# Pooling six key chunks of one batch by row sums, one of them on GpSimd, and one more GELU chunk on VectorE, in a kernel of attention and a feed-forward layer

## The chip, the cores and the metric

The kernel runs on one core of a Trainium2 chip. The metric is device time in microseconds of one execution; lower is better. Three runs of the kernel before took 941.83, 941.97 and 942.03 us, so its median is 941.97 us.

## The reference

Attention with spatially reduced keys, followed by a feed-forward layer with a fast GELU (all inputs float32):

```python
# q (4, 12288, 128), kv (4, 384, 32, 128), w_sr (128, 128)
kv_pool = kv.reshape(B, H // 4, 4, W // 4, 4, C).mean(axis=(2, 4))
k = v = kv_pool.reshape(B, -1, C) @ w_sr            # 768 keys in each batch
a = softmax(q @ k.T / sqrt(C));  x = a @ v          # 49152 tokens of 128
h = x @ w_in                                        # d_ff = 2048
out = (h * sigmoid(1.702 * h)) @ w_out
```

## The kernel before

**Tiles.** The 49152 tokens are cut into 96 groups of 512. A group of attention has 6 chunks of 128 keys (`JC`), a group of the feed-forward layer ("MoE" in the names) 16 chunks of 128 hidden units (`FCH`). A *chunk* is always a 128x512 piece: TensorE makes it in PSUM by one matmul of 512 columns (a *fill*: L404 in attention, L690 in MoE), ScalarE puts three chunks (two at the start) through exp or GELU in one ACTIVATE (L406, L692) and writes them in bf16 into a ring `ag` of 102 chunks, and TensorE reads them back (a *drain*: L418 in attention, 4 matmuls of 129 columns a chunk, and L700 in MoE, one matmul of 512 columns). The ring lets drains lag behind fills by many chunks. Normalised attention outputs (L446, L449 on VectorE) go into the SBUF tile `x`, tile by tile of 2048 columns, to DRAM and back transposed.

**Order.** The program runs attention of groups 0 to 47, MoE of 0 to 47, attention of 48 to 95, MoE of 48 to 95. A planner in Python (the loop at the end, with `now`, `end`, `free`, `dve`) writes out one fixed order for every engine: in each step it fills the next two or three chunks, and then puts drains and small jobs (`extras`, `early_fill`) into TensorE's queue as long as by its costs they fit ahead of the next fill. Each engine works its queue in that order, and waits on semaphores where data is not there.

**Chunks that ScalarE does not do.** 36 exp chunks and the 27 GELU chunks of `lent` are computed on VectorE by polynomials (`early_exp`, `lent_gelu`: 16 VectorE instructions for one GELU chunk) out of a bank that one fill (L475) wrote; the result lies in `aside` and is drained like any other. Of the 27, six are of the first MoE (groups 3, 6, 7, 10, 12, 18).

**Keys of batch 1**, around the change. Each of its six key chunks is a [128, 2048] piece of `kv`, loaded by GpSimd's DMA queue (`load_chunk`, three at group 10, three at group 12). The 4x4 pooling of a chunk is done in one of two ways.

- *In rows*: chunks 0 to 4 (`ADDED`) are loaded as float32 into borrowed homes of 4 KB a partition and more (`homes`: the tile `kvs`, the tile `w_both` of the weights to come, and pairs of tiles of `x`). `add_row` sums them on VectorE in three adds (two at L165, float32, 512 elements a partition; one at L167, to bf16), and `pool_added` then does four small matmuls against `sum4` (L178).
- *By TensorE alone*: chunk 5 is loaded as bf16 into one tile of `x`, and `pool_chunk` does sixteen such matmuls (L154).

`SUM` says at which group each chunk's sums begin. Behind either way stands `key_and_value` (L199, L200), which needs the pooled chunk. GpSimd works one queue: gates (a MEMSET at L600 that waits for one of VectorE, so that loads aren't issued too early), DMA issues (L142, L145, L248), and, for the first 30 token tiles, the normalising multiply (L449).

Of the kernel before, what the change touches and what calls it, by code (L numbers as in the profile page):

```python
# [7 lines left out]
F32 = mybir.dt.float32  # L8
F32R = mybir.dt.float32r
I32 = mybir.dt.int32  # L10
BF = mybir.dt.bfloat16
AF = mybir.ActivationFunctionType
AX = mybir.AxisListType
ADD = mybir.AluOpType.add
# [12 lines left out]
def kernel(  # L27
    ctx, tc, q, kv, w_sr, moe_w_in, moe_w_out, out,
):
    nc = tc.nc  # L30
    B, N, C = q.shape
    _, H, W, _ = kv.shape
    r = 4
# [4 lines left out]
    FCH = d_ff // 128  # L38
    scale = 1.0 / (C ** 0.5)
    G = 512  # L40
    SG = 4 * G
# [21 lines left out]
    R = 2  # L63
    XS = NS // R
    EARLY = 4
    ADDED = (0, 1, 2, 3, 4)
    AG = 102

    cpool = ctx.enter_context(tc.tile_pool(name="const", bufs=1))
# [20 lines left out]
    def acc(key=None):  # L90

        nonlocal last_acc
        last_acc = next_acc()
        turns.append(last_acc)
        turns.remove(last_acc)
        if key:
            closes[last_acc] = key
        return banks[:, last_acc, :]
# [15 lines left out]
    x = xpool.tile([128, XS * SG], BF, name="x")  # L114

    def x_tile(s):
        return x[:, s % XS * SG:(s % XS + 1) * SG]
# [5 lines left out]
    kv_tiles, kv_sums, pooled, pTs, kTs, vs, added = {}, {}, {}, {}, {}, {}, {}  # L123
    kvs = kvsum.tile([128, 2, Wp, C], F32, name="kvs")
    w_both = cpool.tile([128, 2 * d_ff], BF, name="w_both")
    homes = [kvs.rearrange("p a w c -> p (a w c)"), w_both.bitcast(F32)]
    homes += [x[:, s * SG:(s + 2) * SG].bitcast(F32) for s in (XS - 6, XS - 4, XS - 2)]
    wide = dict(zip(ADDED, homes))
    plain = [jc for jc in range(JC) if jc not in wide]
    spots = {jc: XS - 1 - (JC if len(wide) == JC - 1 else k) for k, jc in enumerate(plain)}  # L130
# [7 lines left out]
    def load_chunk(b, jc):  # L138

        a, ch = divmod(jc, HC)  # L140
        if b and jc in wide:
            nc.gpsimd.dma_start(out=wide[jc], in_=kv_r[b, a, ch])  # L142
            return
        t = x_tile(spots[jc] if b else XS - 1 - jc)
        nc.gpsimd.dma_start(out=t, in_=kv_r[b, a, ch])  # L145
        kv_tiles[b, jc] = t.rearrange("p (wp w1 c) -> p w1 wp c", w1=r, c=C)

    def pool_chunk(b, jc):

        ps = acc()  # L150
        t = kv_tiles.pop((b, jc))
        for wp in (0, 2, 1, 3) if (b, jc) == (0, 0) else range(4):
            for w in range(r):
                nc.tensor.matmul(ps[:, 32 * wp:32 * wp + 32], t[:, w, wp, :], sum4,  # L154
                                 start=(w == 0), stop=(w == r - 1))
        pTs[b, jc] = kvtmp.tile([128, 128], BF, name="pTc", bufs=2)
        nc.vector.tensor_copy(pTs[b, jc], ps[:, 0:128])

    def add_row(jc):

        last, wp = False, None
        t = wide[jc].rearrange("p (wp e) -> p wp e", wp=r)
        narrow_sum = wide[jc].bitcast(BF).rearrange("p (wp e) -> p wp e", wp=r)[:, :, 4 * C:5 * C]
        for m in (0, 2):
            nc.vector.tensor_tensor(t[:, m:m + 2, 0:2 * C], t[:, m:m + 2, 0:2 * C], t[:, m:m + 2, 2 * C:4 * C], ADD)  # L165
            yield 3.2
        nc.vector.tensor_tensor(narrow_sum, t[:, :, 0:C], t[:, :, C:2 * C], ADD)  # L167
        added[jc] = narrow_sum
        extras.extend([(pool_added, 1, jc), (key_and_value, 1, jc)])
        last = True  # L170
        yield 3.3
# [34 lines left out]
    def add_kv(b, n):  # L206
        i, w = divmod(n, r)
        if n == 0:
            kv_sums[b] = kvs[0:Hp]
        for i2 in range(2):  # L210
            nc.gpsimd.dma_start(out=kv_sums[b][:, i2], in_=kv_p[b, i, w, :, i2],  # L211
                                **({"accum_op": ADD} if n else {}))
# [33 lines left out]
    def cast_q(s, lo=0):  # L246
        sl = slice(s * SG + lo * G, (s + 1) * SG)
        nc.gpsimd.dma_start(out=q_bf[sl, :].rearrange("(p i) c -> p (i c)", p=128),  # L248
                            in_=q_flat[sl, :].rearrange("(p i) c -> p (i c)", p=128))

    def load_qT(s):
        qTs[s] = qpool.tile([128, 1, SG], BF, name="qT")
        nc.vector.memset(qTs[s][:, 0, 0:1], 0.0)
        nc.sync.dma_start_transpose(out=qTs[s], in_=q_bf[s * SG:(s + 1) * SG, :])


    def load_rest(s, lo):
        qTs[s] = qpool.tile([128, 1, SG], BF, name="qT")
        nc.vector.memset(qTs[s][:, 0, lo * G:lo * G + 1], 0.0)
        nc.sync.dma_start_transpose(out=qTs[s][:, :, lo * G:], in_=q_bf[s * SG + lo * G:(s + 1) * SG, :])  # L260
# [59 lines left out]
    for m in range(0, 128, 32):  # L320
        p = slice(m, m + 32)
# [60 lines left out]

    early = range(NG // R, NG // R + EARLY)
    rolling = [(i, JC - 1) for i in (28, 41, 42, 55, 59, 64, 70, 71, 74, 85, 91, 94)]
    lent = [(g, FCH - 1) for g in (3, 6, 7, 10, 12, 18, 52, 54, 56, 57, 61, 62, 64, 67, 68, 71, 73, 75, 77, 79, 82, 84, 85, 88, 90, 92, 93)]
    turn = [("a",) + c for c in rolling if c[0] < early[0]] + [("m",) + c for c in lent if c[0] < early[0]]
    turn += [("a",) + c for c in rolling if c[0] > early[-1]] + [("m",) + c for c in lent if c[0] > early[-1]]
    aside = agpool.tile([128, K, 512], BF, name="aside")
# [96 lines left out]
    def new_raw():  # L485
        nonlocal raw
        raw = qpool.tile([128, 1, SG], BF, name="qT")[:, 0, 0:2 * G].bitcast(F32)
# [89 lines left out]
    def put_away(n, m):  # L577
        size = PART // 2 if n == 0 and m > FIRST + 1 else PART
        for o in range(m * PART, m * PART + PART, size):
            lo = n * XS * SG + o * T  # L580
            nc.sync.dma_start(out=x_bf[lo:lo + size * T, :].rearrange("(k p) c -> p k c", p=T),
                              in_=x[:, o * T:(o + size) * T].rearrange("p (k c) -> p k c", k=size))

    def bring_back(n, m):
        o = m * PART
        lo = n * XS * SG + o * T
        nc.sync.dma_start_transpose(out=x[:, o * T:(o + PART) * T].unsqueeze(1), in_=x_bf[lo:lo + PART * T, :])
# [7 lines left out]
    def gate():  # L595

        one = gate_tile[:, gates[0] % 8:gates[0] % 8 + 1]
        gates[0] += 1
        nc.vector.memset(one, 0.0)  # L599
        nc.gpsimd.memset(one, 0.0)  # L600
# [6 lines left out]
    def background(i):  # L607

        first_round = i < GB * 2
        s = TURN.get(i, NS) if first_round else i // 4 + 3 if i % 4 == 0 else NS  # L610
        if s < NS:
            load_qT(s)
        if i == 5:
            load_rest(2, 2)
        if i in CAST:
            gate()
            for s in CAST[i]:
                cast_q(s)
        if i in (10, 12):
            gate()  # L620
            for jc in range(i % 10 * 3 // 2, i % 10 * 3 // 2 + 3):
                load_chunk(1, jc)
        for jc in SUM.get(i, ()):
            if jc in wide:
                sums.append(add_row(jc))
            else:
                extras.extend([(pool_chunk, 1, jc), (key_and_value, 1, jc)])
        if i in (28, 33, 38):
            put_away(0, (i - 28) // 5)
        if i in (31, 36, 41):  # L630
            bring_back(0, (i - 31) // 5)
        if i == 40:
            new_raw()
        if 4 * XS - LEAD <= i < 4 * XS:
            gate()
            add_kv(2, i - 4 * XS + LEAD)
        if i == 28:
            gate()
            nc.gpsimd.dma_start(out=w_in_sb, in_=moe_w_in)
        if i == 29:  # L640
            gate()
            nc.gpsimd.dma_start(out=w_out_sb, in_=moe_w_out.rearrange("(o p) c -> p o c", p=128))

    def background_moe(g):
# [16 lines left out]
        if g == 43:  # L661
            raw = None
            background(early[0])
# [19 lines left out]
    extras = []  # L683
# [66 lines left out]
    for n in range(R):  # L750
        part = [c for c in chunks if c[0] // (NG // R) == n]
        while part:
            m = sizes.pop(0) if sizes else K
# [12 lines left out]
        while flat:  # L766
            m = K if len(flat) > sum(rest) else rest.pop(0)
# [36 lines left out]
    def prepare(p):  # L804
# [12 lines left out]

    first = {
        0: [(pool_chunk, 0, 0), (transpose_q, 0), (warm, 1), (key_chunk, 0, 0), (transpose_q, 1)],
        1: [(value_chunk, 0, 0), (warm, 1)],  # L820
        2: [(pool_chunk, 0, 1), (warm, 2), (key_and_value, 0, 1), (warm, 1), (transpose_q, 2)],
        3: [(transpose_q, 3), (transpose_q, 4), (transpose_q, 5)],
        6: [(pool_chunk, 0, 2)],
# [65 lines left out]
    for n in range(len(seq)):  # L889
        fill(n + 2)  # L890
        jobs(n + 3)
        while True:
# [37 lines left out]
            kind, i, c = source[0]  # L930
# [58 lines left out]
```

## Time and profile before

| what | us |
|---|---|
| median of 3 runs | 941.97 |
| the profiled execution | 942.05 |
| its span, first to last instruction | 940.3 |
| TensorE busy | 928.5 |
| ScalarE busy | 927.7 |
| VectorE busy | 620.3 |
| GpSimd busy | 76.0 |

The profiled execution took 942.05 us, 1.75 us more than its span and 0.08 us more than the median. TensorE's and ScalarE's rows both read 99%; what that means is taken up stage by stage below. Groups in the profile are named by line, engine and operation; "128x1024" is 128 partitions by 1024 elements, so two chunks.

### The profile page before, as it was taken

How to read it: one execution, taken by the hardware profiler on the slowest of the kernel's cores; microseconds unless marked ns; L12 is line 12 of the kernel's file. 1: busy time of each engine (PE TensorE's matmuls, PEld its weight loads, DVE VectorE, ACT ScalarE, POOL GpSimd, SP SyncE). 2: the span in 40 equal slices, each digit the busy share in tenths (PEclk: the TensorE clock that was granted, in tenths of full speed). 3: DMA queues.
4: the chain of work that ended last, by engine and by line, in shares of the span. 5: the costliest groups of instructions: out<-in, count | busy, mean ns of one | idle time of the engine just before them, and what ended most of it. 6: DMA issues, size and time to landing. Idle time of an engine off the chain costs nothing.

```text
span 940.3 us, 15356 instructions
## 1 busy us (share of the span) xinstructions
PE 928.5 (99%) x6103; PEld 499.7 (53%) x6218; DVE 620.3 (66%) x1244; ACT 927.7 (99%) x721; POOL 76.0 (8%) x129
## 2 busy tenths in 40 slices
PE   8999999999999999999999999999999999999998
PEld 5777775444444444454447777744444444444444
DVE  6776556685288777777036767457587778577781
ACT  6999999999999999999999999999999999999998
POOL 4401014200004320000000000000000000000000
PEclk9999999999999999999999999999999999999999
DMA  9998989937689992775334965471221222222122
GB/s 210 222 286 177 170 175 128 140 69 161 146 143 172 167 129 39 116 127 96 62 60 99 172 132 116 88 135 34 40 40 34 45 35 43 37 40 40 33 46 45
DMA packets 379511, 99.91 MB, mean 106 GB/s; under 512 B 353584, under 2 KB 377008, under 8 KB 378320
## 3 DMA queue, kind: packets, MB, share of 16 engines
q1 hardware_dynamic: 350928, 64.13, 36.8%
q0 software_dynamic: 28368, 34.74, 22.2%
q8 instruction: 48, 0.79, 0.4%
q14 instruction: 23, 0.19, 0.1%
q10 hardware_dynamic: 144, 0.07, 0.0%
HBM read 52.49 MB, written 49.81 MB: 109 GB/s over the span
## 4 chain that ended last, share of the span: by engine, by line
PE 97%; DVE 1%; issue 1%; DMA 1%; POOL 0%; POOLq 0%
PE banks L700 34%; PE banks L690 34%; PE banks L418 14%; PE banks L404 12%; PE banks L481 1%; DMA x<-in_kv_dram 1%; PE banks L475 1%; PE banks L728 0%; PE banks L154 0%; DVE eb L515 0%; DVE ee L513 0%; DVE eb L511 0%; PE banks L280 0%; DVE qT L286 0%; POOL x L266 0%
## 5 line engine op out<-in xcount | busy, mean ns | idle before, releaser
L692 ACT ACTIVATE ag<-banks 128x1536 bf16<-128x1536 f32 (+1 forms) x506 | 676.4, 1496 | 0.0
L690 PE MATMUL banks<-x,w_both 128*128 128x512 bf16 x1460 | 402.4, 379 | 1.8
L700 PE MATMUL banks<-ag,w_both 128*128 128x512 bf16 x1475 | 402.4, 379 | 1.6
L406 ACT ACTIVATE ag<-banks 128x1536 bf16<-128x1536 f32 (+2 forms) x207 | 244.4, 1352 | 3.5 <-PE banks L280 2.3
L700 PEld LDWEIGHTS <-w_both 128*128 128x128 bf16 x1520 | 148.6, 98 | 178.5
L690 PEld LDWEIGHTS <-w_both 128*128 128x128 bf16 x1509 | 146.6, 98 | 172.0 <-issue 0.2
L418 PEld LDWEIGHTS <-ag 128*128 128x128 bf16 x2256 | 147.1, 98 | 48.9 <-issue 0.2
L418 PE MATMUL banks<-v,ag 128*128 128x129 bf16 x2256 | 166.8, 220 | 0.7
L711 DVE STREAM_TRANSPOSE o_sb<-banks 128x512 f32<-128x512 f32 x95 | 67.9, 715 | 144.7 <-PE banks L700 141.8
L404 PE MATMUL banks<-qT,kT 128*128 128x512 bf16 x493 | 144.9, 379 | 1.8 <-DVE kT L187 0.2
L449 DVE TENSOR_TENSOR x<-banks,rec 128x384 bf16<-128x384 f32 x118 | 65.8, 558 | 4.1
L446 DVE RECIPROCAL rec<-banks 128x3 f32<-128x3 f32 x118 | 21.1, 179 | 69.7 <-PE banks L418 69.4
L404 PEld LDWEIGHTS <-kT 128*128 128x128 bf16 x540 | 45.2, 98 | 18.2 <-issue 0.6
L211 POOL DMA_DIRECT2D kvs<-in_kv_dram x32 | 40.8, 1277 | 56.0 <-DMA kvs<-in_kv_dram 55.2
L515 DVE SCALAR_TENSOR_TENSOR eb<-ea 128x512 f32<-128x512 f32 x63 | 43.5, 691 | 1.9
L511 DVE SCALAR_TENSOR_TENSOR eb<-ea 128x512 f32<-128x512 f32 x63 | 43.5, 691 | 1.9
L513 DVE SCALAR_TENSOR_TENSOR ee<-eb,ee 128x512 f32<-128x512 f32 x63 | 43.4, 689 | 1.8
L521 DVE TENSOR_SCALAR ea<-banks 128x512 f32<-128x512 f32 x36 | 24.9, 692 | 29.6 <-PE banks L481 29.4
L713 POOL DMA_DIRECT2D out_dram<-o_sb x2 | 1.3, 672 | 513.1 <-DVE o_sb L711 513.1
L532 DVE TENSOR_SCALAR qT<-banks 128x512 f32<-128x512 f32 x27 | 18.7, 691 | 29.8 <-PE banks L475 29.8
L600 POOL MEMSET gate_tile<- 1x1 f32 x38 | 8.3, 219 | 263.0 <-DVE gate_tile L599 263.0
L504 DVE TENSOR_SCALAR ea<-ea 128x512 int32<-128x512 f32 x63 | 27.7, 440 | 2.0
(96 smaller groups left out, 418.3 us busy)
## 6 DMA issues: line engine op xcount, KB each, us to landing
out_dram<-o_sb SPq DMA_DIRECT2D x379, 64.0 KB, 1.9
kvs<-in_kv_dram POOLq DMA_DIRECT2D x32, 384.0 KB, 6.8
q_bf<-in_q_dram POOLq DMA_DIRECT2D x21, 512.0 KB, 9.1
x_bf<-x SPq DMA_DIRECT2D x13, 768.0 KB, 5.7
x<-in_kv_dram POOLq DMA_DIRECT2D x6, 512.0 KB, 11.6
x<-in_kv_dram POOLq DMA_DIRECT2D x3, 1024.0 KB, 11.5
x_bf<-x SPq DMA_DIRECT2D x6, 384.0 KB, 4.6
x<-in_kv_dram SPq DMA_DIRECT2D x1, 1024.0 KB, 5.1
```

The source lines that it names most:

```text
L211: nc.gpsimd.dma_start(out=kv_sums[b][:, i2], in_=kv_p[b, i, w, :, i2], **({"accum_op": ADD} if n else {}))
L404: nc.tensor.matmul(ps[:, k, :], kTs[i // GB][:, jc * 128:(jc + 1) * 128], rhs, start=True, stop=True)
L406: nc.scalar.activation(place([("a",) + c for c in chunks]), ps, AF.Exp, scale=scale)
L418: nc.tensor.matmul(av_of[u][:, k * (C + 1):(k + 1) * (C + 1)], weights(("a", i, jc))[:, o:o + T], vs[i // GB][:, jc, 0:C + 1], start=(jc = ...
L449: (nc.gpsimd if split else nc.vector).tensor_tensor(to, ps[:, :, 0:C], rec.unsqueeze(2).broadcast_to([128, TS, C]), MUL)
L511: nc.vector.scalar_tensor_tensor(b, a, P2[0], a, ADD, MUL)
L513: nc.vector.scalar_tensor_tensor(e, b, P2[1], e, ADD, MUL)
L515: nc.vector.scalar_tensor_tensor(b, a, P2[2], a, ADD, MUL)
L690: nc.tensor.matmul(ps[:, k, :], w_in_sb[:, fc * 128:(fc + 1) * 128], x[:, g % (4 * XS) * G:(g % (4 * XS) + 1) * G], start=True, stop=True)
L692: nc.scalar.activation(place([("m",) + c for c in chunks]), ps, AF.Gelu_apprx_sigmoid)
L700: nc.tensor.matmul(o_of[g], w_out_sb[:, fc, :], weights(("m", g, fc)), start=(fc == 0), stop=(fc == FCH - 1))
L711: nc.vector.transpose(o_sb, o_of.pop(g))
```

## The change

Three things, with the diff below.

1. Chunk 5 of batch 1 is added in rows too. All six loads are now float32, and the homes are dealt out anew: chunks 0 to 3 in pairs of tiles of `x`, 4 in `w_both`, 5 in `kvs`.
2. Chunk 3's three adds are issued to GpSimd (`add_aside`, at group 17) in place of VectorE, and its `pool_added` and `key_and_value` are queued for TensorE at once.
3. Chunk 15 of group 15 of the first MoE joins `lent`: VectorE does its GELU.

```diff
-    ADDED = (0, 1, 2, 3, 4)
+    ADDED = (0, 1, 2, 3, 4, 5)
...
-    homes = [kvs.rearrange("p a w c -> p (a w c)"), w_both.bitcast(F32)]
-    homes += [x[:, s * SG:(s + 2) * SG].bitcast(F32) for s in (XS - 6, XS - 4, XS - 2)]
+    homes = [x[:, s * SG:(s + 2) * SG].bitcast(F32) for s in (XS - 8, XS - 6, XS - 4, XS - 2)]
+    homes += [w_both.bitcast(F32), kvs.rearrange("p a w c -> p (a w c)")]
...
+    ASIDE = {17: (3,)}
+
+    def add_aside(jc):
+
+        t = wide[jc].rearrange("p (wp e) -> p wp e", wp=r)
+        narrow_sum = wide[jc].bitcast(BF).rearrange("p (wp e) -> p wp e", wp=r)[:, :, 4 * C:5 * C]
+        for m in (0, 2):
+            nc.gpsimd.tensor_tensor(t[:, m:m + 2, 0:2 * C], t[:, m:m + 2, 0:2 * C], t[:, m:m + 2, 2 * C:4 * C], ADD)
+        nc.gpsimd.tensor_tensor(narrow_sum, t[:, :, 0:C], t[:, :, C:2 * C], ADD)
+        added[jc] = narrow_sum
...
-    lent = [(g, FCH - 1) for g in (3, 6, 7, 10, 12, 18, 52, ...
+    lent = [(g, FCH - 1) for g in (3, 6, 7, 10, 12, 15, 18, 52, ...
...
+        for jc in ASIDE.get(i, ()):
+            add_aside(jc)
         for jc in SUM.get(i, ()):
-            if jc in wide:
+            if jc in added:
+                extras.extend([(pool_added, 1, jc), (key_and_value, 1, jc)])
+            elif jc in wide:
                 sums.append(add_row(jc))
```

The planner's order moves with it. Line numbers above L155 shift in the changed kernel (L178 is L189, L404 is L415, L418 is L429, L600 is L611, L692 is L707).

**TensorE, chunk 5.** Before, its pooling is sixteen pairs of weight load and matmul between two steps of attention (ten of the rows here; the left-out ones are the same pair again):

```order
L404 MATMUL banks<-qT,kT 128x512
L154 LDWEIGHTS x [waits DMASW6_49]
L154 MATMUL banks<-sum_126,x 128x32
...
L154 LDWEIGHTS x
L154 MATMUL banks<-sum_126,x 128x32
L404 LDWEIGHTS kT
L404 MATMUL banks<-qT,kT 128x512 [waits Activation_49]
```

They are gone. Chunk 5 now has four such pairs a little later, which wait for the load and for VectorE's adds:

```order
L429 LDWEIGHTS ag
L429 MATMUL banks<-v,ag 128x129
L189 LDWEIGHTS kvs [waits DMASW6_49,DVE_49]
L189 MATMUL banks<-sum_126,kvs 128x32
L189 LDWEIGHTS kvs
L189 MATMUL banks<-sum_126,kvs 128x32
...
L429 LDWEIGHTS ag
```

TensorE has 24 rows fewer in all (12414 against 12438), 12 matmuls and 12 weight loads.

**TensorE and GpSimd, chunk 3.** At the step of attention behind chunk 1's keys, TensorE had two fills and then nine drains (two of their rows here) up to the next fill:

```order
L404 MATMUL banks<-qT,kT 128x512 [waits Activation_49]
L404 LDWEIGHTS kT
L404 MATMUL banks<-qT,kT 128x512
L418 LDWEIGHTS ag
L418 MATMUL banks<-v,ag 128x129
...
L404 LDWEIGHTS kT
```

Now chunk 3's four pooling matmuls stand there, three drains behind the fills; the first waits for the load and for GpSimd:

```order
L415 MATMUL banks<-qT,kT 128x512 [waits Activation_49]
L415 LDWEIGHTS kT
L415 MATMUL banks<-qT,kT 128x512
L429 LDWEIGHTS ag
...
L429 MATMUL banks<-v,ag 128x129
L189 LDWEIGHTS x [waits DMASW4_49,Pool_49]
L189 MATMUL banks<-sum_126,x 128x32
...
L429 LDWEIGHTS ag
```

On GpSimd the gate and cast of group 16 (`q_bf` is the bf16 copy of q in DRAM) were followed by those of group 26:

```order
L600 MEMSET gate_tile 1x1 [waits DVE_49]
L248 DMA q_bf<-in_q_dram 16x16384 [waits DMASW2_49]
L600 MEMSET gate_tile 1x1 [waits DVE_49]
L248 DMA q_bf<-in_q_dram 16x16384 [waits DMASW3_49]
L248 DMA q_bf<-in_q_dram 16x16384 [waits DMASW4_49]
```

Between the two the three adds stand now; the first waits for chunk 3's load, the last for the two before it:

```order
L611 MEMSET gate_tile 1x1 [waits DVE_49]
L259 DMA q_bf<-in_q_dram 16x16384 [waits DMASW2_49]
L166 TENSOR_TENSOR x<-x 128x2x256 [waits DMASW4_49]
L166 TENSOR_TENSOR x<-x 128x2x256
L167 TENSOR_TENSOR x<-x 128x4x128 [waits Pool_49]
L611 MEMSET gate_tile 1x1 [waits DVE_49]
L259 DMA q_bf<-in_q_dram 16x16384 [waits DMASW3_49]
```

**ScalarE and VectorE, the GELU chunk.** ScalarE's whole first MoE before and after; the stage loses one chunk, so its last instruction is one of two chunks:

```order
L406 ACTIVATE ag<-banks 128x1536 x43
L692 ACT_TABLE_LOAD
L692 ACTIVATE ag<-banks 128x1536 x254
L406 ACT_TABLE_LOAD
L406 ACTIVATE ag<-banks 128x1536 x85
```

```order
L417 ACTIVATE ag<-banks 128x1536 x43
L707 ACT_TABLE_LOAD
L707 ACTIVATE ag<-banks 128x1536 x253
L707 ACTIVATE ag<-banks 128x1024
L417 ACT_TABLE_LOAD
L417 ACTIVATE ag<-banks 128x1536 x85
```

On VectorE the new chunk's 16 instructions start directly behind the second copy of batch 2's keys (L240 before). There, before, stood only the transposes of outputs (L711) up to the next lent chunk's first instruction:

```order
L552 TENSOR_SCALAR aside<-qT,eb 128x512 [waits DVE_49]
L711 STREAM_TRANSPOSE o_sb<-banks 128x512 [waits DMAHW2_49,DMAHW1_49,DMAHW7_49,DMAHW0_49,PE_49]
L240 COPY kT<-banks 128x384 [waits PE_49]
L711 STREAM_TRANSPOSE o_sb<-banks 128x512 [waits DMAHW6_49,DMAHW5_49,DMAHW7_49,DMAHW4_49,PE_49]
L711 STREAM_TRANSPOSE o_sb<-banks 128x512 [waits DMAHW3_49,DMAHW4_49,DMAHW2_49,DMAHW5_49,DVE_49,PE_49]
L711 STREAM_TRANSPOSE o_sb<-banks 128x512 [waits DMAHW1_49,DMAHW2_49,DMAHW0_49,DMAHW7_49,DVE_49,PE_49]
L532 TENSOR_SCALAR qT<-banks 128x512 [waits PE_49]
```

```order
L563 TENSOR_SCALAR aside<-qT,eb 128x512 [waits DVE_49]
L726 STREAM_TRANSPOSE o_sb<-banks 128x512 [waits DMAHW2_49,DMAHW1_49,DMAHW7_49,DMAHW0_49,PE_49]
L251 COPY kT<-banks 128x384 [waits PE_49]
L543 TENSOR_SCALAR qT<-banks 128x512 [waits PE_49]
L545 TENSOR_SCALAR ea<-qT 128x512 [waits DVE_49]
L515 TENSOR_SCALAR ea<-ea 128x512 [waits DVE_49]
L518 TENSOR_SCALAR ee<-ea 128x512 [waits DVE_49]
```

The last four rows are the first of the new chunk's sixteen; the transposes now lie between its instructions and behind them, ahead of the next lent chunk. (Operations with a scalar and two tensors read TENSOR_SCALAR in these rows and SCALAR_TENSOR_TENSOR in the profile.)

More of the change, by code (lines that the diff above doesn't have):

```diff
@@ L384 @@
     rolling = [(i, JC - 1) for i in (28, 41, 42, 55, 59, 64, 70, 71, 74, 85, 91, 94)]
-    lent = [(g, FCH - 1) for g in (3, 6, 7, 10, 12, 18, 52, 54, 56, 57, 61, 62, 64, 67, 68, 71, 73, 75, 77, 79, 82, 84, 85, 88, 90, 92, 93)]
+    lent = [(g, FCH - 1) for g in (3, 6, 7, 10, 12, 15, 18, 52, 54, 56, 57, 61, 62, 64, 67, 68, 71, 73, 75, 77, 79, 82, 84, 85, 88, 90, 92, 93)]
     turn = [("a",) + c for c in rolling if c[0] < early[0]] + [("m",) + c for c in lent if c[0] < early[0]]
```

## The prediction

> **What bounds the kernel now.** I read the page's busy rows first, then the chain of waits by engine, then the table of stages.
>
> ```profile
> PE 928.5 (99%) x6103; PEld 499.7 (53%) x6218; DVE 620.3 (66%) x1244; ACT 927.7 (99%) x721; POOL 76.0 (8%) x129
> ...
> PE 97%; DVE 1%; issue 1%; DMA 1%; POOL 0%; POOLq 0%
> ...
> 45.00:90.00 45.00, 44.47 (x518) 32.96 (x525) 32.73 (x96) 45.00 (x47) 5.69 (x19) 1.00 0.92 238
> 145.00:300.00 155.00, 154.26 (x732) 71.41 (x745) 98.46 (x176) 155.00 (x117) 20.96 (x28) 1.00 0.85 137
> 610.00:900.00 290.00, 288.58 (x1323) 131.63 (x1349) 212.38 (x357) 290.00 (x217) 0.00 (x0) 1.00 0.26 46
> ```
>
> The stage rows are: length, then busy time and count of TensorE, weight loads, VectorE, ScalarE and GpSimd, the granted clock (1.00) and the DMA share. ScalarE is busy in every microsecond of all three stages. TensorE misses half a per cent, and those are gaps of one matmul record each: its weight loads show 1349 instructions where its matmuls show 1323. The list of waits for 45 to 935 us has no entry for TensorE and none for ScalarE. So two engines are full at once, and neither waits for the other. VectorE (66%) and GpSimd (8%) are not.
>
> The rate of ScalarE follows from one row of its timeline, and from its groups by form:
>
> ```profile
> 142.76 341.35 ACT L692 ACTIVATE ag<-banks 128x1536 bf16<-128x1536 f32 x254
> ...
> L406 ACT ACTIVATE ag<-banks 128x1536 bf16<-128x1536 f32 x128 | 172.2, 1540 | 0.0
> ...
> L406 ACT ACTIVATE ag<-banks 128x1024 bf16<-128x1024 f32 x77 | 71.0, 1058 | 2.7 <-PE banks L280 2.3 <-PE banks L404 0.4
> ```
>
> 341.35 / 254 = 1.344 us per instruction of three chunks through the whole first MoE; attention has the same, 172.2 / 128 = 1.345. Two chunks take 71.0 / 77 = 0.922. A chunk less in an instruction is therefore worth 1.345 - 0.922 = 0.42 us of ScalarE. (The mean of one, 1540 ns, overlaps its neighbours and is not the rate.)
>
> With both full, the end moves only as far as the engine that gains *less*. That is the rule by which I add up.
>
> **The change part by part.**
>
> *Chunk 5 in rows: TensorE.* The rows are from TensorE's timeline: a pooling in the row form, and chunk 5's by TensorE alone, each with what starts behind it.
>
> ```profile
> 70.33 0.25 PE L178 MATMUL banks<-sum,x 128*128 128x32 bf16 x4
> 70.43 0.67 PE L418 MATMUL banks<-v,ag 128*128 128x129 bf16 x9
> ...
> 72.25 0.56 PE L154 MATMUL banks<-sum,x 128*128 128x32 bf16 x16
> 72.65 0.38 PE L404 MATMUL banks<-qT,kT 128*128 128x512 bf16 x1
> ```
>
> Start to start, four matmuls occupy 70.43 - 70.33 = 0.10 us and sixteen 72.65 - 72.25 = 0.40 us. Twelve fewer save **0.30 us** of TensorE. Nothing else on TensorE is removed: the lent chunk keeps its fill and its drain.
>
> *Chunk 5 in rows: the load.* It is now 1024 KB written instead of 512 KB. The issues and landings (GpSimd's timeline, the DMA issues at 44.42, 45.53 and 48.21 us):
>
> ```profile
> 44.42 1.12 POOL L142 DMA_DIRECT2D x<-in_kv_dram  x2
> 45.53 0.55 POOL L145 DMA_DIRECT2D x<-in_kv_dram  x1
> ...
> x<-in_kv_dram POOLq DMA_DIRECT2D x1, 1024.0 KB, 11.5
> ...
> x<-in_kv_dram POOLq DMA_DIRECT2D x1, 1024.0 KB, 13.4
> x<-in_kv_dram POOLq DMA_DIRECT2D x1, 512.0 KB, 15.2
> ...
> q_bf<-in_q_dram POOLq DMA_DIRECT2D x1, 512.0 KB, 15.0
> ```
>
> Chunk 3 lands at 44.42 + 11.5 = 55.9 us, chunk 4 near 44.97 + 13.4 = 58.4, chunk 5 at 45.53 + 15.2 = 60.7, the next cast at 48.21 + 15.0 = 63.2. A float32 chunk takes 2.5 us of the queue, the cast one 2.3: it lands 0.2 us later, and its first use, behind chunk 4's, is about 10 us off. I cost it at nothing. If the doubled bytes cost a whole chunk's time (2.5 us), still nothing waits.
>
> *Chunk 5's three adds on VectorE* replace chunk 3's three, which leave it. Nothing changes in sum.
>
> *Chunk 3 on GpSimd* is the part that adds a wait to a full engine, so both sides are worked out.
>
> ```profile
> 36.52 4.75 POOL L449 TENSOR_TENSOR x<-ag,sums 128x384 bf16<-128x384 f32 x6 [0.21 <-DVE sums L446]
> ...
> 56.45 0.49 POOL L248 DMA_DIRECT2D q_bf<-in_q_dram  x1
> ...
> 60.66 0.59 PE L404 MATMUL banks<-qT,kT 128*128 128x512 bf16 x2
> 61.09 0.67 PE L418 MATMUL banks<-v,ag 128*128 128x129 bf16 x9
> 61.60 0.59 PE L404 MATMUL banks<-qT,kT 128*128 128x512 bf16 x2
> ```
>
> GpSimd is free at 56.45 + 0.49 = 56.94, and the data is there since 55.9. Its adds of 512 float32 elements are not in this trace; the nearest row is its multiply of 384, six in 4.75 us with the last one's 0.83 us overlapping: (4.75 - 0.83) / 5 = 0.785 each, 2.04 ns an element, so 1.05 us for 512. Three take 3.1, plus about 0.1 for the wait of the third: done at 60.2. TensorE gets there after the two fills and three of nine drains: 61.09 + 3 x 0.057 = 61.26. **1.0 us to spare: nothing.** From below, GpSimd could be as fast as VectorE's 0.60 (its rows below: 49.70 to 50.30) and be done at 58.9, also worth nothing. From above, at twice my duration it would be done at 63.3 and stop TensorE for 2.1 us. I take the nearest row, 1.05. Behind the adds on GpSimd stands only the cast of group 26, which went out at 83 us.
>
> VectorE runs adds of the same kind meanwhile:
>
> ```profile
> 49.70 0.69 DVE L165 TENSOR_TENSOR kvs<-kvs 128x512 f32<-128x512 f32 x1
> ...
> 50.30 0.69 DVE L165 TENSOR_TENSOR kvs<-kvs 128x512 f32<-128x512 f32 x1
> ...
> 57.91 0.68 DVE L167 TENSOR_TENSOR w_both<-w_both 128x512 bf16<-128x512 f32 x1
> 58.51 0.68 DVE L165 TENSOR_TENSOR x<-x 128x512 f32<-128x512 f32 x1
> ...
> 59.50 0.26 PE L178 MATMUL banks<-sum,w_both 128*128 128x32 bf16 x4
> ```
>
> Two of them, at 57.91 and 58.51, fall into GpSimd's stretch; the first feeds TensorE's pooling at 59.50, with 59.50 - 58.59 = 0.9 us to spare. In this trace GpSimd's multiplies met no VectorE instruction with two inputs in SBUF, so it cannot show whether the two disturb each other; that is a rival below.
>
> *The lent GELU chunk.* ScalarE loses **0.42 us** (254 instructions of three become 253 and one of two). VectorE gains sixteen instructions of 0.41 to 0.69 us, under 16 x 0.69 = 11 us, at the place where the timeline shows it nearly idle:
>
> ```profile
> 225.43 0.65 DVE L552 SCALAR_TENSOR_TENSOR aside<-qT,eb 128x512 bf16<-128x512 f32 x1
> 231.47 0.72 DVE L711 STREAM_TRANSPOSE o_sb<-banks 128x512 f32<-128x512 f32 x1 [5.40 <-PE banks L700]
> ...
> 238.33 0.72 DVE L711 STREAM_TRANSPOSE o_sb<-banks 128x512 f32<-128x512 f32 x1 [5.05 <-PE banks L700]
> 245.02 0.72 DVE L711 STREAM_TRANSPOSE o_sb<-banks 128x512 f32<-128x512 f32 x1 [5.97 <-PE banks L700]
> ...
> 255.81 0.69 DVE L532 TENSOR_SCALAR qT<-banks 128x512 f32<-128x512 f32 x1 [3.38 <-PE banks L475]
> ...
> L700 PE MATMUL banks<-aside,w_both x4: 379/379/379, 196.4 to 237.9; 128*128 128x512 bf16 x4
> ```
>
> Between 226 and 256 us it does little but four transposes. The lent chunk whose last instruction starts at 225.43 is drained only at 237.9 (the last of the four drains from `aside` between 195 and 260 us), 11.8 us after its end, so one more fits in front of its own drain. I cost it at nothing. If VectorE were as full there as it is elsewhere, the eleven microseconds would come late, and those 11.8 would still cover them.
>
> *The sum.* TensorE -0.30, ScalarE -0.42; the end follows the smaller: 942.05 - 0.30 = 941.75 for the profiled execution, which stands 0.08 over the median, so 941.67. I say **941.7 us**, 0.03% less: below the 0.2% (1.9 us) that I take as about what a measurement of this kernel tells from no change.
>
> **A rule of the skill against it.** The rows at 57.91 and 58.51 are adds with both inputs in SBUF. The Trainium skill, "SBUF — State Buffer", says under "Who interferes with whom" that such a VectorE instruction contends with a GpSimd one that reads SBUF, the later one blocking until the other is finished. By that rule the second rival decides and the sum is 0.14 to 1.2 us more; without it the forecast stands. No run so far shows which.
>
> **The rivals.**
>
> 1. *ScalarE alone sets the pace*, TensorE's fullness being only its order. Then the gain is 0.42 us: 941.55. For it: ScalarE's rate is the same 1.344 in both kinds of stage. Against: the chain of waits is TensorE's for 97%, without a wait. 0.10.
> 2. *The two adders hold each other up* (the side that is not faster than before). If GpSimd waits for both VectorE adds, it ends at 60.2 + 2 x 0.60 = 61.4, and TensorE stops for 0.14 us: 941.8. If VectorE waits instead, for two GpSimd adds, its 57.91 add ends 2.1 us later, at 60.7, and TensorE's pooling of chunk 1 at 59.50 stops for 1.2 us: +0.9 net, 942.6. It makes the kernel slower from a stop of 0.30 us on, by 0.2% only from 2.2 us. For it: the places really coincide. Against: a few tenths of overlap are all that is needed to get past each other. 0.25.
> 3. *Much slower GpSimd adds* (in place, strided, float32 out): from 2.2 us each the stop is 2.2 us, 943.8 and more. The nearest row is half that. 0.04.
> 4. *It doesn't do what it says*: ScalarE's and TensorE's gains come at 72 and at 480 us, and if the buffers between give the first back, the time stays: 942.0. 0.08.
> 5. *A new order has a hole elsewhere* (the planner's costs, not the chip's, set it): 0.3 to 2 us. 0.05.
>
> **How the numbers follow.** The forecast has the remaining 0.48 and lies at 941.5 to 941.9 by the spread of the three runs (0.2 us). The likeliest case gives 941.7. With rivals 1, 2 and 4 it covers nine tenths, so 941.4 to 942.6 leaves out rivals 3, most of 5 and the edge. Faster by over 0.2% (under 940.1) has no mechanism among these: 0.02. Slower by over 0.2% (over 943.9): rival 3 and the tail of 5, 0.05. Within: 0.93.
>
> **What the changed profile would show.** GpSimd's three adds near 57.0 to 60.2 us, each about 1.05; the first L189 matmul on `x` behind them near 61.26 with no wait; ScalarE 253 + 1 instructions in the first MoE, still without a gap; TensorE's and ScalarE's entries in the list of waits still none; the sixteen lent instructions between 227 and 250 us; each later stage starting about 0.3 us earlier. A wait of TensorE at L189 for GpSimd or VectorE refutes the 1.0 us to spare; a gap on ScalarE at the end of the first MoE says that TensorE alone sets the end; a change of more than 1 us either way would mean that the two full engines are not what bounds it.

## The result, and the profile after

The changed kernel took **943.87 us**, median of 15 runs (943.23 to 945.55), beside 942.03 us for the kernel before in as many runs on the same chip (941.81 to 942.30): 1.84 us more, ratio 1.0020, 95% interval 1.0012 to 1.0028. The forecast was 941.7 with a range to 942.6: wrong side, and 1.3 us outside. The profiled execution took 944.09 us, with a span of 942.3.

I read the stages first. These are the seven microseconds in which GpSimd's adds run, by the table of stages; columns as in the prediction. Before:

```profile
57.00:64.00 7.00, 6.95 (x84) 5.11 (x83) 5.59 (x15) 7.00 (x8) 0.00 (x0) 1.00 1.22 263
```

And after:

```profile
57.00:64.00 7.00, 5.08 (x64) 3.61 (x62) 6.18 (x10) 5.07 (x7) 4.22 (x4) 1.00 1.25 318
64.00:90.00 26.00, 26.00 (x300) 18.93 (x298) 20.11 (x58) 26.00 (x28) 1.67 (x5) 1.00 0.80 157
```

Both full engines lose 1.9 us here together: TensorE goes from 6.95 to 5.08, ScalarE from 7.00 to 5.07, and GpSimd is busy 4.22 us where it did nothing. From 64 us on both are full again. VectorE does ten instructions in 6.18 us where it did fifteen in 5.59: each takes longer. The list of waits of the changed kernel (engine, line, what it waited for; total us, times, longest us) from 30 to 940 us has three lines for ScalarE and for TensorE's matmuls that were not there before:

```profile
ACT ag L417 <- PE banks L415: 1.9, 2, 1.5
...
PE banks L210 <- DVE pTc L191: 1.5, 1, 1.5
...
PE banks L189 <- DVE x L178: 0.4, 1, 0.4
```

TensorE twice waits for VectorE, never for GpSimd; ScalarE's 1.9 us are TensorE's, handed on. GpSimd's timeline of the changed kernel (start, length, then what; "x2" is two instructions in one row):

```profile
57.12 2.51 POOL L166 TENSOR_TENSOR x<-x 128x512 f32<-128x512 f32 x2
59.70 1.61 POOL L167 TENSOR_TENSOR x<-x 128x512 bf16<-128x512 f32 x1
```

VectorE's timeline beside it:

```profile
57.60 0.56 DVE L460 TENSOR_TENSOR x<-banks,rec 128x384 bf16<-128x384 f32 x1
58.08 2.11 DVE L178 TENSOR_TENSOR x<-x 128x512 bf16<-128x512 f32 x1
60.11 1.76 DVE L176 TENSOR_TENSOR x<-x 128x512 f32<-128x512 f32 x1
61.79 0.17 DVE L457 RECIPROCAL rec<-banks 128x3 f32<-128x3 f32 x1
61.99 0.56 DVE L460 TENSOR_TENSOR x<-banks,rec 128x384 bf16<-128x384 f32 x1
62.46 0.28 DVE L191 CAST pTc<-banks 128x128 bf16<-128x128 f32 x1
```

The two VectorE adds that took 0.68 us each before now take 2.11 and 1.76. Their ends give the reason away: GpSimd's first two adds end at 57.12 + 2.51 = 59.63, VectorE's first at 58.08 + 2.11 = 60.19, which is 0.56 later. GpSimd's third ends at 59.70 + 1.61 = 61.31, VectorE's second at 60.11 + 1.76 = 61.87, again 0.56 later. TensorE's timeline shows who waits for them (in brackets the idle time, and for whom):

```profile
60.24 0.27 PE L189 MATMUL banks<-sum,x 128*128 128x32 bf16 x4 [0.41 <-DVE x L178]
60.36 0.33 PE L429 MATMUL banks<-v,ag 128*128 128x129 bf16 x3
60.52 0.59 PE L415 MATMUL banks<-qT,kT 128*128 128x512 bf16 x2
60.95 0.33 PE L429 MATMUL banks<-v,ag 128*128 128x129 bf16 x3
62.80 0.22 PE L210 MATMUL banks<-pTc,w_sr_sb 128*128 128x128 bf16 x1 [1.51 <-DVE pTc L191]
...
63.68 0.25 PE L189 MATMUL banks<-sum,x 128*128 128x32 bf16 x4
```

The first stop is the pooling of chunk 1, which needs the first blocked add. The second, larger one is the matmul for chunk 1's keys. It needs the copy L191 of the pooled chunk, which has nothing to do with the second blocked add but stands behind it in VectorE's queue, and starts only at 62.46. Chunk 3's own pooling, the one that needs GpSimd, comes at 63.68, 2.4 us after GpSimd is done.

The chain of waits by engine, which read TensorE 97% before, now reads:

```profile
ACT 51%; PE 47%; DMA 1%; DVE 1%; issue 0%; POOL 0%; POOLq 0%
```

This looks like a change of the bound, but it doesn't go with the time: of the runs below, the one with a median of 941.63 us reads ACT 51% as well, and the one with 944.24 us reads PE 97%. With both engines full, the chain can be followed back through either.

### The profile page after: what moved, and what is told of

It is laid out like the page before. It is cut to its first block, busy times and chain, and to the rows that moved or that the text cites. A ratio compares the mean times of both kernels' runs of the same rounds, so it can differ in the third digit from the quotient of the medians.

```text
span 942.3 us, 15470 instructions
## 1 busy us (share of the span) xinstructions
PE 934.5 (99%) x6206; PEld 499.3 (53%) x6206; DVE 631.3 (67%) x1260; ACT 927.7 (98%) x721; POOL 80.5 (9%) x132
## 4 chain that ended last, share of the span: by engine, by line
ACT 51%; PE 47%; DMA 1%; DVE 1%; issue 0%; POOL 0%; POOLq 0%
ACT ag L707 36%; PE banks L715 17%; PE banks L705 17%; ACT ag L417 14%; PE banks L429 6%; PE banks L415 5%; DMA x<-in_kv_dram 1%; PE banks L486 0%; PE banks L743 0%; PE banks L154 0%; DVE x L178 0%; DVE x L176 0%; DVE qT L297 0%; ACT L417 0%; ACT L707 0%
## 5 line engine op out<-in xcount | busy, mean ns | idle before, releaser
L707 ACT ACTIVATE ag<-banks 128x1536 bf16<-128x1536 f32 (+1 forms) x506 | 676.1, 1472 | 0.0
L705 PE MATMUL banks<-x,w_both 128*128 128x512 bf16 x1508 | 408.0, 379 | 0.0
L429 PEld LDWEIGHTS <-ag 128*128 128x128 bf16 x2256 | 147.4, 98 | 48.9 <-issue 0.2
L429 PE MATMUL banks<-v,ag 128*128 128x129 bf16 x2256 | 167.5, 220 | 0.0
L415 PE MATMUL banks<-qT,kT 128*128 128x512 bf16 x540 | 150.3, 379 | 0.3 <-DVE kT L198 0.2
L460 DVE TENSOR_TENSOR x<-banks,rec 128x384 bf16<-128x384 f32 x118 | 65.8, 558 | 4.1
L415 PEld LDWEIGHTS <-kT 128*128 128x128 bf16 x540 | 45.0, 98 | 18.3 <-issue 1.0
L611 POOL MEMSET gate_tile<- 1x1 f32 x38 | 8.1, 212 | 264.2 <-DVE gate_tile L610 257.8
```

Source lines behind the costliest of these rows:

```text
L415: nc.tensor.matmul(ps[:, k, :], kTs[i // GB][:, jc * 128:(jc + 1) * 128], rhs, start=True, stop=True)
L429: nc.tensor.matmul(av_of[u][:, k * (C + 1):(k + 1) * (C + 1)], weights(("a", i, jc))[:, o:o + T], vs[i // GB][:, jc, 0:C + 1], start=(jc = ...
L460: (nc.gpsimd if split else nc.vector).tensor_tensor(to, ps[:, :, 0:C], rec.unsqueeze(2).broadcast_to([128, TS, C]), MUL)
L705: nc.tensor.matmul(ps[:, k, :], w_in_sb[:, fc * 128:(fc + 1) * 128], x[:, g % (4 * XS) * G:(g % (4 * XS) + 1) * G], start=True, stop=True)
L707: nc.scalar.activation(place([("m",) + c for c in chunks]), ps, AF.Gelu_apprx_sigmoid)
```

## The experiments

Theory: *lock*. While a GpSimd add runs, a VectorE add with both inputs in SBUF stands still; the two stops of TensorE come from that alone. Rivals: *crowding* (the adds would be late in the new order anyhow, with or without GpSimd); *lateness* (GpSimd's adds are simply too slow for their place); *the new order* (it has a hole of its own). Ratios are against the kernel before, on the same chip in the same session.

### Three writes in place of the three adds

```diff
         for m in (0, 2):
-            nc.gpsimd.tensor_tensor(t[:, m:m + 2, 0:2 * C], t[:, m:m + 2, 0:2 * C], t[:, m:m + 2, 2 * C:4 * C], ADD)
-        nc.gpsimd.tensor_tensor(narrow_sum, t[:, :, 0:C], t[:, :, C:2 * C], ADD)
+            nc.gpsimd.memset(t[:, m:m + 2, 0:2 * C], 0.0)
+        nc.gpsimd.memset(narrow_sum, 0.0)
```

This leaves out the sums of chunk 3 (its keys are zeros); TensorE's order is row for row that of the changed kernel.

> The changed kernel with GpSimd's three adds replaced by three MEMSETs over the same outputs, so that chunk 3's keys are zeros; order and semaphores are the same, but GpSimd reads nothing from SBUF. Lock theory: VectorE's adds at 58.1 and 60.1 us are back at 0.68 us, no stop of TensorE, 941.6 to 941.9. Crowding: the same order on VectorE gives the same stops, 943.5 or over. If GpSimd's writes also held VectorE, its adds would be longer by the MEMSETs' durations, and the time lies between.

Measured: **941.63 us** (941.44 to 941.91), ratio 0.9995 (0.9986 to 1.0004). GpSimd's timeline in it:

```profile
57.12 1.02 POOL L166 MEMSET x<- 128x512 f32 x2
58.19 0.52 POOL L167 MEMSET x<- 128x512 bf16 x1
```

VectorE's and TensorE's:

```profile
58.10 0.68 DVE L178 TENSOR_TENSOR x<-x 128x512 bf16<-128x512 f32 x1
58.70 0.69 DVE L176 TENSOR_TENSOR x<-x 128x512 f32<-128x512 f32 x1
...
59.99 0.29 DVE L191 CAST pTc<-banks 128x128 bf16<-128x128 f32 x1
```

```profile
59.70 0.26 PE L189 MATMUL banks<-sum,x 128*128 128x32 bf16 x4
...
60.57 0.22 PE L210 MATMUL banks<-pTc,w_sr_sb 128*128 128x128 bf16 x1
...
61.45 0.26 PE L189 MATMUL banks<-sum,x 128*128 128x32 bf16 x4
```

The third write runs from 58.19 to 58.71, wholly beside an add that starts at 58.10: that add takes 0.68, as without a neighbour. All stops are gone. Chunk 1's pooling and keys come 0.54 and 2.23 us earlier than in the changed kernel; 941.63 + 2.23 = 943.86, beside the 943.87 measured (closer than either kernel's own runs agree). So the whole loss is the two stops, and what remains of the change is a gain of 0.4 us, which the interval does not tell from none.

The same without the lent chunk (the list `lent` as before):

> As the run in which GpSimd only writes (chunk 3's keys are zeros), without the lent GELU chunk: no stop, TensorE -0.30, ScalarE unchanged. If the end follows the engine that gains less: 942.0. If TensorE alone sets the end: 941.6, the same as with the lent chunk.

Measured: 942.25 us (942.04 to 942.34), ratio 1.0002 (0.9993 to 1.0011). The list of waits has no line for TensorE between 30 and 930 us in either. Each is within its interval of no change. Their runs don't overlap, on two chips on which the kernel before had 942.02 and 942.05: TensorE's 0.30 us alone bought nothing, and with ScalarE's 0.42 beside it the kernel is 0.6 us faster. That is more than either gain, so it supports the rule of the smaller gain (0.30) by its direction, not by its size.

### Only chunk 3 on GpSimd

The kernel before with `ASIDE = {17: (3,)}` and `add_aside`; chunk 5 by TensorE and six lent chunks, as before.

> The kernel before with chunk 3's adds on GpSimd and nothing else: chunk 5 stays with TensorE, old homes, no lent chunk. Lock theory: both stops and no saving, 2.1 to 2.3 us over before, 944.1 to 944.4. Rival, homes and loads (the loss comes from the new homes or the larger load of chunk 5): 942.0 to 942.3.

Measured: 944.24 us (943.32 to 946.45), ratio 1.0025 (1.0013 to 1.0037), as expected, though its six runs spread over 3 us. The rows are from the longest, of 946.45 us, which has TensorE's two stops as in the changed kernel and longer stops of ScalarE between 60 and 67 us. GpSimd, then VectorE:

```profile
56.86 2.50 POOL L166 TENSOR_TENSOR x<-x 128x512 f32<-128x512 f32 x2
59.44 1.61 POOL L167 TENSOR_TENSOR x<-x 128x512 bf16<-128x512 f32 x1
```

```profile
57.82 2.10 DVE L178 TENSOR_TENSOR w_both<-w_both 128x512 bf16<-128x512 f32 x1
59.84 1.75 DVE L176 TENSOR_TENSOR x<-x 128x512 f32<-128x512 f32 x1
```

The same pattern with other tiles: here VectorE's first add works on `w_both`, GpSimd on `x`. It is not the tile that is shared. By the medians, this one part carries the whole loss: 944.24 - 942.02 = 2.22 us.

### GpSimd reads one input

```diff
-            nc.gpsimd.tensor_tensor(t[:, m:m + 2, 0:2 * C], t[:, m:m + 2, 0:2 * C], t[:, m:m + 2, 2 * C:4 * C], ADD)
-        nc.gpsimd.tensor_tensor(narrow_sum, t[:, :, 0:C], t[:, :, C:2 * C], ADD)
+            nc.gpsimd.tensor_copy(t[:, m:m + 2, 0:2 * C], t[:, m:m + 2, 2 * C:4 * C])
+        nc.gpsimd.tensor_copy(narrow_sum, t[:, :, 0:C])
```

Chunk 3's sums leave out three of each four terms.

> The changed kernel with GpSimd's three adds replaced by three copies of the same sizes, so that chunk 3's sums leave terms out; they read SBUF through one input instead of two. If any SBUF read by GpSimd stops VectorE's two-input adds, the adds at 58.1 and 60.1 us are longer by about the part of a copy that they meet, up to a microsecond each; if only GpSimd's two-input instructions do, they stay at 0.68 us and the time is 941.7.

Measured, in one run: 941.85 us. GpSimd, then VectorE:

```profile
56.88 1.17 POOL L166 COPY x<-x 128x512 f32<-128x512 f32 x2
58.11 0.96 POOL L167 CAST x<-x 128x512 bf16<-128x512 f32 x1
```

```profile
57.86 0.74 DVE L178 TENSOR_TENSOR x<-x 128x512 bf16<-128x512 f32 x1
58.52 1.09 DVE L176 TENSOR_TENSOR x<-x 128x512 f32<-128x512 f32 x1
```

GpSimd's instructions end at 58.05 and 59.07, VectorE's at 58.60 and 59.61: again 0.55 and 0.54 later. The second add took 1.09 us in place of 0.68. So reading one input is enough to hold VectorE. The copies are merely too short to stop TensorE.

### The same adds in eight pieces

```diff
-        for m in (0, 2):
...
+        for m in range(r):
+            nc.gpsimd.tensor_tensor(t[:, m, 0:2 * C], t[:, m, 0:2 * C], t[:, m, 2 * C:4 * C], ADD)
+            nc.gpsimd.tensor_tensor(narrow_sum[:, m, :], t[:, m, 0:C], t[:, m, C:2 * C], ADD)
```

> The changed kernel with GpSimd's three adds of 512 elements cut into eight (four of 256 and four of 128, each pair dependent through a semaphore), at the same place. Lock theory: VectorE can get in behind each short piece, so its adds at 58.1 and 60.1 us stand still for one piece (0.3 to 0.6 us) instead of two whole adds; TensorE's stop at 59.5 goes or falls under 0.2 us, the one at chunk 3's keys falls to 1 us or less: 942.3 to 943.2. If GpSimd, once started, keeps VectorE out until its queue is empty: as the changed kernel or worse, 943.9 and over.

Measured: 943.34 us (943.17 to 943.50), ratio 1.0014 (1.0005 to 1.0023), just above the range. TensorE's timeline:

```profile
60.77 0.22 PE L210 MATMUL banks<-pTc,w_sr_sb 128*128 128x128 bf16 x1 [0.35 <-DVE pTc L191]
...
62.96 0.19 PE L189 MATMUL banks<-sum,x 128*128 128x32 bf16 x1 [1.08 <-POOL x L167]
```

Now VectorE gets in between the pieces and the first stop is gone. But GpSimd waits in turn (three of its pieces are longer than their like), and even free pieces add up to 4.7 us (four of 0.72 and four of 0.46), where the three whole adds take 3.8. It ends at 62.9, and TensorE stops for GpSimd itself. Here, small pieces only move the wait.

### The same adds at another place

The adds gated behind VectorE's last add of chunk 2, and chunk 3's pooling queued behind chunk 4's; TensorE's order is otherwise the changed kernel's:

```diff
-    ASIDE = {17: (3,)}
+    ASIDE = {}
...
         extras.extend([(pool_added, 1, jc), (key_and_value, 1, jc)])
         last = True
+        if jc == 2:
+            gate()
+            add_aside(3)
...
-    SUM = {14: (0,), 15: (1,), 16: (2,), 17: (3,), 20: (4,), 21: (5,)}
+    SUM = {14: (0,), 15: (1,), 16: (2,), 20: (4,), 21: (3, 5)}
```

> The changed kernel with chunk 3's three GpSimd adds gated behind VectorE's last add of chunk 2, and chunk 3's pooling queued behind chunk 4's; TensorE's order is the changed one but for that, up to 78 us. Lock theory: GpSimd's adds start near 63.9, where VectorE has no add of its own until 67.4, last 3.8 us at 1.25 each and end near 67.7; chunk 4's first add waits a few tenths (about 1.3 in place of 0.68) and TensorE does not stop: the gain that the three writes in place of adds showed comes back, 941.6 to 941.9. Rival, that GpSimd's adds cost TensorE time wherever they stand (by SBUF or by their lateness): 942.5 to 944.

Measured: **941.92 us** (941.68 to 942.03), ratio 0.9997 (0.9988 to 1.0006). GpSimd, then VectorE:

```profile
63.17 2.49 POOL L166 TENSOR_TENSOR x<-x 128x512 f32<-128x512 f32 x2
65.74 1.27 POOL L167 TENSOR_TENSOR x<-x 128x512 bf16<-128x512 f32 x1
```

```profile
66.56 0.99 DVE L176 TENSOR_TENSOR w_both<-w_both 128x512 f32<-128x512 f32 x1
67.48 0.68 DVE L176 TENSOR_TENSOR w_both<-w_both 128x512 f32<-128x512 f32 x1
```

One add is held for 0.3 us (its end, 67.55, is 0.54 behind GpSimd's 67.01), and TensorE has no stop. The time is 0.02 us over the expected range. The same three adds cost nothing that can be told here, and this is the fastest complete version of the change; it does not beat the kernel before by anything that can be told. Next, on the same order of TensorE, the gate stands a few VectorE instructions later (`ASIDE = {19: (3,)}` with a `gate()` ahead of `add_aside`):

> The same order on TensorE as the run before, with the gate two VectorE instructions later, near 65.1. Lock theory: GpSimd's adds run from 65.2 to 69.0 and meet chunk 4's two first adds, due at 67.4 and 68.1; these end near 69.6 and 70.2, the third near 71.5, and TensorE's pooling of chunk 4, due near 70.4, stops for about 1.1 us: 942.5 to 943.0. Rival, that the place does not matter: the same time as the run before, within 0.3.

Measured: 942.42 us (942.26 to 942.48), ratio 1.0003 (0.9994 to 1.0011), a little under the expected range. Its runs lie 0.5 us above the ones of the other place, without overlap. GpSimd and VectorE, then TensorE:

```profile
64.40 2.49 POOL L166 TENSOR_TENSOR x<-x 128x512 f32<-128x512 f32 x2
66.96 1.60 POOL L167 TENSOR_TENSOR x<-x 128x512 bf16<-128x512 f32 x1
```

```profile
66.58 0.86 DVE L176 TENSOR_TENSOR w_both<-w_both 128x512 f32<-128x512 f32 x1
67.36 1.75 DVE L176 TENSOR_TENSOR w_both<-w_both 128x512 f32<-128x512 f32 x1
```

```profile
71.94 0.22 PE L210 MATMUL banks<-pTc,w_sr_sb 128*128 128x128 bf16 x1 [0.43 <-DVE pTc L191]
```

I had put the stop at chunk 4's pooling, and at 1.1 us; that pooling was just in time, and the matmul for its keys came at 71.94 where the other place has 71.34, 0.6 later. Once more it is L191, behind late adds in VectorE's queue. Moving GpSimd by 1.2 us, with TensorE's order the same, sets whether it stops.

### Variants without that collision, and a second loss

All three adds of every chunk on VectorE (`ASIDE = {}`, and the planner's two numbers for a step of sums, 3.3 to 3.2 and the allowance 3.0 to 6.0; the expectation names other numbers, 2.8 and groups 18 and 19, which this run does not have):

> The changed kernel with all six chunks added on VectorE, GpSimd adding none (the sums of chunks 4 and 5 begin at groups 18 and 19 and the planner's cost of an add is 2.8, so that the sixth chunk fits). Lock theory (a VectorE add with both inputs in SBUF stands still while a GpSimd add runs, and the whole loss is TensorE's two stops behind that, 0.6 and 1.5 us): no stop, TensorE -0.30, ScalarE -0.42, so 941.6 to 941.8, 0.3 under before. Rival, crowding (VectorE is too full for a sixth chunk in this stretch, whoever adds): stops of a microsecond or more remain, 943 or over.

Measured: 944.87 us (944.61 to 945.18), ratio 1.0029 (1.0019 to 1.0040). The lock theory's number was missed. Nothing stops near 60 us, but chunk 5's sums now come last of eighteen adds on one engine. The list of waits:

```profile
PE banks L210 <- DVE pTc L191: 0.6, 2, 0.4
PE banks L415 <- ACT ag L417: 0.3, 1, 0.3
PE banks L415 <- DVE kT L212: 0.2, 1, 0.2
```

All but 0.2 us of these stand between 80 and 84 us, at the first use of chunk 5's keys. So crowding is real in this form, but it is only about half of the 2.85 us: the first attention ends 1.3 us later than in the run with the writes (142.84 against 141.58), and the rest is the second loss, at the end of this part. Crowding isn't what the changed kernel shows, whose TensorE matmuls have no wait there. The same version without the lent chunk could not be built, and gave no time.

Chunk 0 on GpSimd in place of chunk 3, early and before VectorE's adds (`ASIDE = {13: (0,)}`, `SUM = {15: (0, 1), 16: (2,), 17: (3,), 20: (4,), 21: (5,)}`):

> The changed kernel with GpSimd adding chunk 0 at group 13 instead of chunk 3 at group 17; VectorE's first add, of chunk 1, then begins only when GpSimd is done, near 52 us. All else as in the changed kernel: real adds, five chunks on VectorE, the lent chunk. Lock theory: nothing to collide with, GpSimd's adds about 1.05 to 1.3 us each, VectorE's 0.68, no stop of TensorE: 941.6 to 941.9. Rival (a sixth chunk's work crowds this stretch or GpSimd adds are bad wherever they stand): 943 or over.

Measured: 944.88 us (944.79 to 945.66), ratio 1.0032 (1.0020 to 1.0044); without the lent chunk 944.83 (944.75 to 944.90), ratio 1.0030 (1.0019 to 1.0042).

> As the run before, without the lent GELU chunk: TensorE -0.30, ScalarE unchanged. If the end follows the engine that gains less: 942.0, the same as before the change. If TensorE alone sets the end: the same time as the run before, 941.7.

GpSimd and VectorE in the former:

```profile
48.85 2.50 POOL L166 TENSOR_TENSOR x<-x 128x512 f32<-128x512 f32 x2
51.44 1.27 POOL L167 TENSOR_TENSOR x<-x 128x512 bf16<-128x512 f32 x1
```

```profile
51.71 1.54 DVE L176 TENSOR_TENSOR x<-x 128x512 f32<-128x512 f32 x1
```

Alone, a GpSimd add takes 2.50 / 2 = 1.25 us and the last 1.27. VectorE is held once (53.25, 0.54 behind 52.71), and TensorE does not stop there. Part of the loss is chunk 5 again, its pooling 0.5 us late at 79.84; the first attention ends 1.6 us later than with the writes (143.21). With cheaper planned sums (2.8 in place of 3.2 and 3.3) and chunks 4 and 5 at groups 18 and 19:

> As the run with GpSimd on chunk 0, but with the planner's cost of a VectorE add at 2.8 (it was 3.2 and 3.3) and the sums of chunks 4 and 5 begun at groups 18 and 19, so that chunk 5's keys come some 2 us before their first use at about 80 us. Real adds throughout. If that run lost its time to late keys at 80 us and to nothing of GpSimd, the stops there go: 2.2 us better, 942.7, and 941.6 to 941.9 if the second attention's order comes out as in the changed kernel. If GpSimd's adds are themselves the cost: 944 or over.

Measured: 943.49 us (943.36 to 943.70), ratio 1.0016 (1.0007 to 1.0024). That lies between the numbers of the expectation. TensorE's matmuls no longer wait for VectorE at 80 us, and the first attention ends at 141.55, as with the writes: the three GpSimd adds cost nothing here. But half of the loss stays. Where it lies, the lent chunk alone shows (the kernel before, with chunk 15 of group 15 added to `lent`, nothing else):

> The kernel before with the lent GELU chunk and nothing else: ScalarE -0.42, TensorE unchanged. If the end follows the engine that gains less, or TensorE alone: 942.0. If ScalarE alone sets the end: 941.6.

Measured: 943.41 us (943.21 to 943.58), ratio 1.0014 (1.0005 to 1.0023); both theories missed. Its list of waits has no line for TensorE's matmuls. The stage from 485 to 600 us (attention of batches 2 and 3), in the kernel before:

```profile
485.00:600.00 115.00, 113.86 (x1218) 81.71 (x1237) 77.62 (x184) 114.97 (x87) 0.00 (x0) 1.00 0.58 121
```

With the lent chunk alone:

```profile
485.00:600.00 115.00, 113.38 (x1194) 80.53 (x1213) 76.62 (x182) 114.97 (x86) 0.00 (x0) 1.00 0.55 117
```

TensorE starts 1213 weight loads where it started 1237 in the same 115 us. The loads for fills are 252 in both; those for attention's drains are 934 in place of 959. So it is not slower: the planner had written another order, with fewer drains between the same fills. Work that is put off has to be done in the end, and the end of the program shows it. ScalarE's last run of GELU and TensorE's last drains, in the kernel before:

```profile
923.62 12.50 ACT L692 ACTIVATE ag<-banks 128x1536 bf16<-128x1536 f32 x12
934.89 2.40 PE L728 MATMUL banks<-w_both,ag 128*128 128x128 bf16 x40
```

With the lent chunk alone:

```profile
924.48 11.15 ACT L692 ACTIVATE ag<-banks 128x1536 bf16<-128x1536 f32 x11
934.83 3.74 PE L728 MATMUL banks<-w_both,ag 128*128 128x128 bf16 x64
```

ScalarE is done 0.5 us earlier (935.63 against 936.12), but behind the last fill TensorE still has 64 drain matmuls where it had 40: 3.74 - 2.40 = 1.34 us, and the run lost 1.38. The rows of the sixth chunk on VectorE and of both runs with the lent chunk and chunk 0 on GpSimd read x64 and 3.74 too (x58 without the lent chunk). The changed kernel, the run with the writes and those with the adds at the two other places read x40 and 2.40: they don't have this loss. Why the planner's loop comes to the one order or the other was not followed up.

## Why the prediction was wrong, point by point

- **Two full engines, the smaller gain counts: not refuted, and not shown to the tenth.** With the collision taken out the kernel ran at 941.63 us (writes) and 941.92 us (real adds at another place), against the 941.7 that I forecast; without the lent chunk the gain was gone. That speaks against TensorE alone as the bound. Against ScalarE alone (rival 1) speaks the lent chunk alone: ScalarE was done 0.5 us earlier and the time was 1.4 us longer, because TensorE's last drains set the end. My last sign, that a change of over 1 us would mean another bound, was too coarse: a stop in the middle of a full engine does the same.
- **The load of chunk 5, and the lent chunk's sixteen VectorE instructions: nothing, as said.** In the changed kernel's list, no TensorE matmul and no ScalarE instruction waits for a DMA or for `aside`.
- **"1.0 us to spare: nothing", chunk 3 on GpSimd: the step that failed.** I set GpSimd's end against TensorE's arrival alone, and priced the adds at nothing. GpSimd's end was indeed early enough, though barely: at 61.31, where an unstopped TensorE would arrive at 61.45 (the third L189 row of the run with writes). My 1.05 us from the multiply of 384 elements was too low; alone an add takes 1.25. But the cost of the step was not at that place. It was 2.23 us, by way of the two VectorE adds beside it.
- **"A few tenths of overlap are all that is needed to get past each other": false, and it is why rival 2 had 0.25 instead of the lead.** GpSimd's two first adds run back to back, and VectorE does not get in between: its add of 58.08 stood through the rest of the first and all of the second. The third GpSimd add waits for GpSimd's own result, and in that pause (59.63 to 59.70) VectorE got in; so that third add took 1.61 in place of 1.27, and then held VectorE's next add. They don't get past each other, they take turns, and here a turn lasted until the other engine paused.
- **Rival 2 had the right mechanism, and its price left out the queue.** It gave 1.2 us at chunk 1's pooling; measured 0.54. It did not name the second add of VectorE as blocked too, nor what stands behind it: RECIPROCAL, L460, and then the copy L191 on which chunk 1's keys hang. With the first stop alone the kernel would be at 941.63 + 0.54 = 942.2, inside my range; the second adds 2.23 - 0.54 = 1.69 and makes it 943.9.
- **The rule that I had quoted held.** The Trainium skill, "SBUF — State Buffer", "Who interferes with whom", has a VectorE instruction with two SBUF inputs contend with a GpSimd one that reads SBUF, the later blocking until the other is finished, and says of one that only writes that it does not. These traces agree: 0.68 us beside the writes, 2.11 and 1.76 beside the adds, and 0.56 beside an add for L460, one of whose two inputs lies in PSUM. They differ in one thing: the add of 58.08 waited for two GpSimd adds in a row, not for one. I gave it a quarter; the trace of before held nothing against it, which is a reason to take the rule, not to doubt it.
- **Rival 5, a hole elsewhere in a new order, did not strike here**, but did in the variants of the last part, in the lent chunk alone for 1.4 us: 0.05 was too little.
- **Rival 3 fell, rival 4 stays open.** GpSimd's adds took 1.25 us, not 2.2. Whether the gains come through to the end (rival 4 says no) is not told: with the collision away the time was 0.4 us under the kernel before with the writes and 0.1 us under it with real adds, both within their intervals of no change.

## What to carry to other kernels

An idle engine is not free when it shares something with a busy one: before a VectorE instruction is moved to GpSimd, list the VectorE instructions with two SBUF inputs that will run in the same microseconds, price each as ending almost a whole instruction after GpSimd's, and then go down VectorE's queue to see who waits for what stands behind. The place decides: the same three adds cost 2.2 us at 57 us and nothing measurable at 63. And where the planner's order moves, look at the far stages and at the last drains too, since a loss can show hundreds of microseconds from the edit.

## What the runs showed of the hardware

- Every VectorE add with two SBUF inputs that met a GpSimd instruction reading SBUF ended 0.54 to 0.56 us after that instruction's end: ten such adds in the rows above, beside GpSimd adds and beside copies, and three in the run with eight pieces (0.55 each). A free one takes 0.68, and 0.60 from start to start. So at most a small part of its work is done while it waits.
- It holds in the other direction too: GpSimd's third add ended 1.12 us after the VectorE add that it met (60.19 to 61.31 in the changed kernel, 67.44 to 68.56 with the late gate), against 1.27 alone.
- A copy with one input on GpSimd took 0.58 us for 512 float32 elements (1.17 / 2), an add with two 1.25, a write 0.51. The multiply of 384 elements, 0.785 by the prediction's row, is 2.0 ns an element; the add is 2.4.
